# An adaptive-layernorm block of linear attention and bilinear feed-forward: reordering prepared operands, sums and loads

## The chip, the cores and the metric

The kernel runs on one core of a Trainium2 chip. The engines of a core work side by side, each through its own list of instructions in order: TensorE (PE; PEld is its weight load), VectorE (DVE), ScalarE (ACT), GpSimd (POOL) and SyncE (SP), which here only issues transfers between memory and the on-chip buffers. The metric is device microseconds (us) of one execution; the number given for a kernel is the median over its runs.

## The reference

All arrays are fp32; there are S = 2048 tokens of D = 512, 32 heads of 16, and F = 1376.

```python
mod = (_silu(c) @ w_mod).reshape(c.shape[0], 6, 1, -1)
sa, ca, ga, sb, cb, gb = (mod[:, 0], ..., mod[:, 5])
h = _layernorm(x) * (1 + ca) + sa
x = x + ga * _A_ref(h, A_wqkv, A_wo)          # linear attention
h = _layernorm(x) * (1 + cb) + sb
x = x + gb * _B_ref(h, B_w_gate, B_w_up, B_w_down)

# _A_ref: phi(t) = where(t > 0, t + 1, exp(t)) + 1e-6
kv = einsum("bhsd,bhse->bhde", phi(k), v);  z = einsum("bhsd->bhd", phi(k))
o = einsum("bhqd,bhde->bhqe", phi(q), kv) / (einsum("bhqd,bhd->bhq", phi(q), z)[..., None] + 1e-6)
# _B_ref: ((h @ w_gate) * (h @ w_up)) @ w_down
```

## The kernel before

Tokens come in four chunks (0 to 3) of four tiles of 128. To keep fp32 accuracy at the speed of the fp32r type, every operand of a matmul is split into a high part (ScalarE rounds it) and a low part (the rest, by VectorE or GpSimd: `split`, lines 195 to 197), and a product is three matmuls: high by high, high by low, low by high.

All tiles of 128 x 512 come from one pool of 94 buffers. Each tile takes a free buffer in the order in which the program is written, and the first instruction that writes it waits until the buffer's former users are through. So moving an allocation in the program changes which buffer it and later tiles get, and what they wait for. The order on each engine is the order of the program; nothing reorders it later.

*The early stage* goes over the 16 token tiles (loop from line 488): keys of the tile two ahead, the tile's part of the key sums on TensorE (L336 to L338), the sum z of all phi(k) on VectorE (L321). The table `extra` hangs further work behind some tiles: the six vectors of w_mod are loaded (`mod_load`, four tiles of 256 KB each) and summed up on VectorE one tile of weights at a time (`mod_part`, L164 and L166), and the four tiles of w_o are loaded and split. The last vector, number 5, scales the feed-forward output. At the end z is split (high on ScalarE, low on GpSimd) and summed over partitions by two matmuls (L185).

*The feed-forward* is a sequence of 19 blocks (`ffn`, `block`), 0 to 7 for chunks 0 and 1, 8 to 18 for chunks 2 and 3, one per 128 columns of F. A block multiplies the two chunks by the gate and up weights at once as a 2 x 2 matrix of halves, with seven products instead of eight. Each is six matmuls at L959. The seven are called in the order of the points at which `block` lets other work in:

```python
times(a, A["a11"], ...)                      # first product, then point "p1"
times(d, A["s1"], ...); copy(p5, d)          # second, "p5"
times(b, A["s2"], ...); copy(c, b); ...      # third, "p6"
times(a, A["a12"], ...)                      # fourth, "p2"
times(c, A["s3"], ...); p5 = c + p5          # fifth, "p7" (addition at L1018)
times(d, A["s4"], ...); u2 = d + u2          # sixth, "p3" (L1022), product with a (L987)
times(c, A["a22"], ...)                      # seventh, "p4", product with p5 (L987)
```

`copy` is ScalarE at L964, out of one accumulator bank into the next or into a tile. The fifth product adds into bank c, so it waits for the copy of the third result into c; the seventh adds into c again, so it waits until VectorE has read the fifth result at L1018. Products of a block that are still to be split into kh and kl (L196, L197) are split behind the next block's first copy. After each block come 24 matmuls of the down projection of earlier blocks (L1039 to L1041) and four additions on VectorE that take their results (evictions, L759). Weights are loaded two blocks ahead at the fifth point, and GpSimd forms their differences (L927) and low parts (L945).

The left operands for chunks 2 and 3 are prepared while blocks 1 to 8 run, by the table `plan`, keyed by block and point. The normalised tiles are written out in pieces and read back (`stow`, `unstow`); `flips` turns 32 x 32 squares on VectorE into the tile `wide` (L829); `turned(k, chunk, name)` scales and shifts one quarter of `wide` on ScalarE (L835) and so makes the *scaled block* `name` of half k: a11 and a12 come from chunk 2, a21 and a22 from chunk 3. `sums` forms on VectorE (L877) s1 = a21 + a22, s3 = a11 - a21, s2 = s1 - a11, s4 = a12 - s2, for each half k = 0, 1. `store` splits an operand and writes both parts to memory (L893); `fetch` reads them back in block 7 (L908); `split_in` splits an operand that stays on chip. The scaling of w_down's rows by the last vector is VectorE at L1104, at the third point.

Of the kernel before, what the change touches and what calls it, by code (L numbers as in the profile page):

```python
# [24 lines left out]
def tile_adaln_block(  # L25
# [12 lines left out]
    nc = tc.nc  # L38
# [3 lines left out]
    KD = D // P  # L42
# [13 lines left out]
    wo_v = wo.rearrange("(k p) n -> k p n", p=P)  # L56
# [18 lines left out]
    def T(p, tag, shape=(P, D), dt=F32, bufs=None):  # L75
        cnt[0] += 1
        return p.tile(list(shape), dt, tag="t" if p is tiles else tag, name=f"{tag}_{cnt[0]}", bufs=bufs)

    def B(tag, shape=(P, D), dt=F32):

        return T(tiles, tag, shape, dt)
# [4 lines left out]
    def bank():  # L86
        return T(ps_w, "bank")
# [25 lines left out]
    def load(src, tag):  # L113
        raw = B(tag, (P, *src.shape[1:]))[:src.shape[0]]
        nc.sync.dma_start(raw, src)
        return raw
# [4 lines left out]
    def load_mod(v):  # L121
        return [load(wm_v[:, k, v * D:(v + 1) * D], "raw") for k in range(KD)]
# [38 lines left out]
    def mod_acc(acc, raws, ks):  # L161
        for k in ks:
            if k == 0:
                nc.vector.tensor_scalar(acc, raws[k], sc[:, 0:1], None, op0=ALU.mult)  # L164
            else:
                nc.vector.scalar_tensor_tensor(acc, raws[k], sc[:, k:k + 1], acc, op0=ALU.mult, op1=ALU.add)  # L166

    def mod_col(acc, ps):

        for b in range(KD):  # L170
            nc.tensor.matmul(ps[:, b:b + 1], acc[:, b * P:(b + 1) * P], ones[:, 0:1], start=True, stop=True)
        return ps

    def col_out(v, ps, add):
        t = consts.tile([P, KD], F32, name=f"col{v}")
        nc.vector.tensor_scalar(t, ps[:, :KD], add, None, op0=ALU.add)
        return t
# [4 lines left out]
    def row_sum(pair):  # L182
        ps = bank()
        for n, x in enumerate(pair):
            nc.tensor.matmul(ps, ones_r, x, start=n == 0, stop=n == 1)  # L185
        return ps

    def mod_row(v, pair):
        ps = row_sum(pair)
        t = consts.tile([P, D], F32, name=f"row{v}")  # L190
        nc.scalar.activation(t, ps, AF.Copy)
        return t


    def split(src, h, l, low=None):
        nc.scalar.activation(h, src, AF.Copy)  # L196
        (low or nc.vector).tensor_tensor(l, src, f32(h), op=ALU.subtract)  # L197

    def split_raw(raw, shape=(P, D), low=None):
        h = B("w", shape, F32R)  # L200
        l = B("w", shape, F32R)
        split(raw, h[:raw.shape[0]], l[:raw.shape[0]], low)
        return h, l
# [255 lines left out]
    rows, cols = {}, {}  # L459
    accs = {}  # L460

    raw_m, raw_o, wo_s = {}, [], []

    def mod_load(*vs):
        raw_m.update({v: load_mod(v) for v in vs})

    def mod_part(v, *ks):
        if 0 in ks:
            accs[v] = B("f")
        mod_acc(accs[v], raw_m[v], ks)  # L470
# [4 lines left out]
             7: lambda: (wv.extend(split_raw(r) for r in raw_v[3:4]),),  # L475
             8: lambda: (mod_part(2, 0, 1), mod_load(3)),
             9: lambda: (mod_part(2, 2, 3), mod_load(4)),
             10: lambda: (pairs.update({2: split_raw(accs[2], low=nc.gpsimd)}), mod_part(3, 0, 1, 2), raw_o.extend(load(wo_v[k], "raw") for k in range(KD)), mod_load(5)),
             11: lambda: (mod_part(3, 3), mod_part(4, 0, 1), rows.update({2: mod_row(2, pairs[2])})),
             12: lambda: (mod_part(4, 2, 3), wo_s.extend(split_raw(x) for x in raw_o[:2]), cols.update({3: col_out(3, mod_col(accs[3], bank()), 0.0)})),  # L480
             13: lambda: (mod_part(5, 0, 1, 2), wo_s.extend(split_raw(x) for x in raw_o[2:]), cols.update({4: col_out(4, mod_col(accs[4], bank()), 1.0)})),
             14: lambda: (mod_part(5, 3),)}
    pairs = {}
# [343 lines left out]
    def flip(ch, *js):  # L827
        for j in js:
            nc.vector.transpose(wide[:, j].rearrange("p (m s i) -> p m s i", m=NQ, i=BL),  # L829
                                blocks.pop((ch, j)).rearrange("p (m i s) -> p m s i", m=NQ, i=BL))  # L830

    def flipped(ch, *ks):
        for k in ks:
            f = B("f")
            nc.scalar.activation(f.rearrange("p (x i) -> p x i", i=BL),  # L835
                                 wide.rearrange("p j (m s i) -> p (j m) s i", m=NQ, i=BL)[:, :, k],
                                 AF.Identity, scale=cb4[:, k:k + 1], bias=sb4[:, k:k + 1])
            blocks[ch, "f", k] = f
# [74 lines left out]
    class Right:  # L913
# [12 lines left out]
        def sums(self, on=None):  # L926
            sub = lambda out, x, y: (on or nc.gpsimd).tensor_tensor(out, x, y, op=ALU.subtract)  # L927
            b11, b12, b21, b22 = self.up[:, 0], self.up[:, 1], self.low[:, 0], self.low[:, 1]
            self.t12, self.t34 = self.tile("t"), self.tile("t")
            sub(self.t12[:, 0], b12, b11)  # L930
            sub(self.t12[:, 1], b22, self.t12[:, 0])
            sub(self.t34[:, 0], b22, b12)
            sub(self.t34[:, 1], b21, self.t12[:, 1])
# [354 lines left out]
    def turned(k, ch, n):  # L1288
        i = k + KH * (n in ("a12", "a22"))
        return lambda: (flipped(ch, i), second[k].get(n))  # L1290

    flips = lambda ch, j: lambda: flip(ch, j)
    sums = lambda k, n: lambda: second[k].sum(n)
    store = lambda k, n: lambda: second[k].aside(stash).split(n)
# [4 lines left out]
        (3, "p3"): [turned(0, 2, "a12")], (3, "p4"): [turned(1, 2, "a11"), lambda: unstow(3)],  # L1299
        (4, "p1"): [turned(1, 2, "a12")], (4, "p5"): [flips(3, 0), store(0, "a11")], (4, "p6"): [flips(3, 1)],  # L1300
        (4, "p3"): [store(0, "a12")], (4, "p4"): [flips(3, 2), store(1, "a11")],
        (5, "p1"): [flips(3, 3), store(1, "a12")], (5, "p5"): [turned(0, 3, "a21")], (5, "p6"): [turned(0, 3, "a22")],
        (5, "p3"): [sums(0, "s1")], (5, "p4"): [sums(0, "s3"), turned(1, 3, "a21")],
        (6, "p1"): [sums(0, "s2"), turned(1, 3, "a22")], (6, "p5"): [sums(0, "s4"), store(0, "s1")],
        (6, "p6"): [sums(1, "s1"), store(0, "s3")], (6, "p3"): [store(0, "s2")], (6, "p4"): [sums(1, "s3")],
        (7, "p1"): [sums(1, "s2"), split_in(1, "s1")], (7, "p5"): [sums(1, "s4"), split_in(0, "s4")],
        (7, "p6"): [split_in(1, "s2")], (7, "p3"): [split_in(1, "s3")], (7, "p4"): [split_in(0, "a22")],
        (8, "p1"): [split_in(1, "s4")], (8, "p5"): [split_in(1, "a22")]})
# [31 lines left out]
```

## Time and profile before

| | us |
|---|---|
| median of 3 runs (564.26 to 564.45) | 564.3 |
| profiled execution | 563.62 |
| its span, first to last instruction | 561.9 |
| TensorE busy | 554.7 |
| VectorE busy | 382.4 |
| ScalarE busy | 280.9 |
| GpSimd busy | 189.5 |

The granted TensorE clock of the profiled execution is 0.999 of full speed. A timeline row has the start in us from the span's start, the time that the row covers, engine, line and operation, the tile written and those read, shapes, and the number of instructions merged into the row; in brackets stands the idle time of the engine just before, and what ended it. A row of a stretch has its bounds, its length, and for each engine the busy time with the number of instructions, then the granted clock, the share of the transfer engines and GB/s. A row of transfers has the number, the size of each and the median time from issue to landing.

### The profile page before, as it was taken

How to read it: one execution, taken by the hardware profiler on the slowest of the kernel's cores; microseconds unless marked ns; L12 is line 12 of the kernel's file. 1: busy time of each engine (PE TensorE's matmuls, PEld its weight loads, DVE VectorE, ACT ScalarE, POOL GpSimd, SP SyncE). 2: the span in 40 equal slices, each digit the busy share in tenths (PEclk: the TensorE clock that was granted, in tenths of full speed). 3: DMA queues.
4: the chain of work that ended last, by engine and by line, in shares of the span. 5: the costliest groups of instructions: out<-in, count | busy, mean ns of one | idle time of the engine just before them, and what ended most of it. 6: DMA issues, size and time to landing. Idle time of an engine off the chain costs nothing. (4 is left out here: it accounts for less than half of the span.)

```text
span 561.9 us, 7305 instructions
## 1 busy us (share of the span) xinstructions
PE 554.7 (99%) x2539; PEld 454.5 (81%) x2539; DVE 382.4 (68%) x629; ACT 280.9 (50%) x503; POOL 189.5 (34%) x195
## 2 busy tenths in 40 slices
PE   8999999999999999999999999999999999999997
PEld 7788888888888778878887887787888888888886
DVE  7896968787969876769877587786444444344435
ACT  4695866456557546354783545554333333334120
POOL 2000000100011300001598665656667446446200
PEclk9999999999999999999999999999999999999999
DMA  8900212400501001814425142491335222200004
GB/s 287 384 2 2 75 52 98 152 0 2 153 3 76 0 1 40 259 37 114 132 69 155 41 168 95 154 341 35 114 112 151 56 58 56 58 19 1 1 0 150
DMA packets 51077, 52.01 MB, mean 93 GB/s; under 512 B 7712, under 2 KB 32544, under 8 KB 51040
## 3 DMA queue, kind: packets, MB, share of 16 engines
q1 hardware_dynamic: 51040, 51.54, 28.9%
q8 instruction: 20, 0.33, 0.2%
q14 instruction: 17, 0.14, 0.1%
HBM read 39.46 MB, written 12.06 MB: 92 GB/s over the span
## 5 line engine op out<-in xcount | busy, mean ns | idle before, releaser
L959 PE MATMUL bank<-h,w 128*128 128x512 f32 (+1 forms) x798 | 185.7, 390 | 1.5 <-ACT bank L964 0.9
L959 PEld LDWEIGHTS bank<-h,w 128*128 128x128 f32 (+1 forms) x798 | 148.1, 186 | 36.1 <-ACT bank L964 2.1
L964 ACT ACTIVATE bank<-bank 128x512 f32<-128x512 f32 (+1 forms) x38 | 22.1, 582 | 136.2 <-PE bank L959 136.2
L759 DVE TENSOR_TENSOR x<-acc,x 128x512 f32<-128x512 f32 (+1 forms) x73 | 48.7, 682 | 49.3 <-PE acc L1041 49.3
L945 POOL TENSOR_TENSOR w<-raw,w 128x256 fp32r<-128x256 f32 (+3 forms) x38 | 42.0, 1105 | 111.1 <-ACT w L938 111.1
L1039 PE MATMUL acc<-w,kh 128*128 128x512 f32 (+2 forms) x154 | 59.6, 387 | 0.0
L1040 PE MATMUL acc<-w,kh 128*128 128x512 f32 (+2 forms) x154 | 59.6, 387 | 0.0
L1041 PE MATMUL acc<-w,kl 128*128 128x512 f32 (+2 forms) x154 | 59.5, 386 | 0.0
L197 POOL TENSOR_TENSOR w<-raw,w 128x512 fp32r<-128x512 f32 (+1 forms) x25 | 35.4, 1418 | 54.3 <-ACT w L196 54.3
L237 POOL TENSOR_TENSOR rstd<-ve,half 128x4 f32<-128x4 f32 (+1 forms) x10 | 10.6, 1060 | 123.2 <-DVE ve L236 121.5
L945 POOL TENSOR_TENSOR w<-t,w 128x512 fp32r<-128x512 f32 (+1 forms) x38 | 48.9, 1308 | 0.0
L197 DVE TENSOR_TENSOR kl<-u,kh 128x512 fp32r<-128x512 f32 (+1 forms) x38 | 26.7, 744 | 31.4 <-ACT kh L196 31.4
L209 PE MATMUL bank<-w,h 128*128 128x512 f32 x104 | 40.8, 392 | 0.0
L211 PE MATMUL bank<-w,h 128*128 128x512 f32 x104 | 40.5, 390 | 0.0
L210 PE MATMUL bank<-w,h 128*128 128x512 f32 x104 | 40.5, 389 | 0.0
L695 PE MATMUL acc<-w,xh 128*128 128x512 f32 x120 | 38.2, 400 | 0.0
L1039 PEld LDWEIGHTS acc<-w,kh 128*128 128x128 f32 (+1 forms) x154 | 28.9, 188 | 6.0
L1040 PEld LDWEIGHTS acc<-w,kh 128*128 128x128 f32 (+1 forms) x154 | 28.9, 188 | 5.9
L1041 PEld LDWEIGHTS acc<-w,kl 128*128 128x128 f32 (+1 forms) x154 | 28.9, 188 | 5.9
L1018 DVE TENSOR_TENSOR u<-bank,u 128x512 f32<-128x512 f32 (+1 forms) x19 | 13.1, 687 | 28.1 <-PE bank L959 20.7
L246 ACT ACTIVATE n<-x,nmr,rstd 128x512 f32<-128x512 f32 x30 | 22.9, 804 | 16.3 <-DVE nmr L240 15.0
L196 ACT ACTIVATE w<-raw 128x512 fp32r<-128x512 f32 (+2 forms) x44 | 26.3, 618 | 1.6 <-DVE raw L739 1.0
(198 smaller groups left out, 1112.9 us busy)
## 6 DMA issues: line engine op xcount, KB each, us to landing
raw<-in_w_mod_dram SPq DMA_DIRECT2D x24, 256.0 KB, 4.0
raw<-in_B_w_down_dram SPq DMA_DIRECT2D x20, 256.0 KB, 2.9
raw<-in_B_w_gate_dram SPq DMA_DIRECT2D x36, 128.0 KB, 3.6
raw<-in_B_w_up_dram SPq DMA_DIRECT2D x36, 128.0 KB, 3.5
x<-in_A_x_dram SPq DMA_DIRECT2D x16, 256.0 KB, 5.2
out_dram<-x SPq DMA_DIRECT2D x15, 256.0 KB, 2.7
raw<-in_A_wqkv_dram SPq DMA_DIRECT2D x12, 256.0 KB, 5.2
kept<-f SPq DMA_DIRECT2D x8, 256.0 KB, 2.0
```

What stands on the lines that cost most here:

```text
L196: nc.scalar.activation(h, src, AF.Copy)
L197: (low or nc.vector).tensor_tensor(l, src, f32(h), op=ALU.subtract)
L209: nc.tensor.matmul(ps, ah, bh, start=i == 0, stop=False)
L210: nc.tensor.matmul(ps, ah, bl, start=False, stop=False)
L211: nc.tensor.matmul(ps, al, bh, start=False, stop=i == n - 1)
L695: nc.tensor.matmul(yps[i], x, y, start=False, stop=k == KD - 1 and x is al, skip_group_check=True)
L759: nc.vector.tensor_tensor(xt[:, a:b], dn[j][:, a:b], xt[:, a:b], op=ALU.add)
L945: sub = lambda out, x, y: (on or nc.gpsimd).tensor_tensor(out, x, f32(y), op=ALU.subtract)
L959: mm = lambda x, y, **kw: nc.tensor.matmul(ps, x[:, k], y, skip_group_check=True, **kw)
L1039: nc.tensor.matmul(ps, hh[:, a:b], dh[:n, c:d], start=i == 0, stop=False)
L1040: nc.tensor.matmul(ps, hh[:, a:b], dl[:n, c:d], start=False, stop=False)
L1041: nc.tensor.matmul(ps, hl[:, a:b], dh[:n, c:d], start=False, stop=i == len(hs) - 1)
```

## The change

Three things are moved; no instruction is added or taken away.

In the early stage the loads of w_o are divided, two tiles behind token tile 10 and two behind tile 11, and the four loads of vector 5 move from tile 10 to tile 12.

In the table `plan`, the scaled blocks a21 and a22 of half 0 are made behind the third and sixth product of block 5 instead of the second and third, and the split and store of a12 of half 1 move from the first point of block 5 to its seventh. The sums of half 0 follow one place later: s1 behind the seventh product of block 5, s3 and s2 behind the first and second of block 6, s4 behind the seventh. The sums s1 and s3 of half 1 stand behind the seventh product of block 6; before, s1 stood behind the third.

```diff
-             10: lambda: (pairs.update({2: split_raw(accs[2], low=nc.gpsimd)}), mod_part(3, 0, 1, 2), raw_o.extend(load(wo_v[k], "raw") for k in range(KD)), mod_load(5)),
-             11: lambda: (mod_part(3, 3), mod_part(4, 0, 1), rows.update({2: mod_row(2, pairs[2])})),
-             12: lambda: (mod_part(4, 2, 3), wo_s.extend(split_raw(x) for x in raw_o[:2]), cols.update({3: col_out(3, mod_col(accs[3], bank()), 0.0)})),
+             10: lambda: (pairs.update({2: split_raw(accs[2], low=nc.gpsimd)}), mod_part(3, 0, 1, 2), raw_o.extend(load(wo_v[k], "raw") for k in range(2))),
+             11: lambda: (mod_part(3, 3), mod_part(4, 0, 1), rows.update({2: mod_row(2, pairs[2])}), raw_o.extend(load(wo_v[k], "raw") for k in range(2, KD))),
+             12: lambda: (mod_part(4, 2, 3), wo_s.extend(split_raw(x) for x in raw_o[:2]), cols.update({3: col_out(3, mod_col(accs[3], bank()), 0.0)}), mod_load(5)),
...
-        (5, "p1"): [flips(3, 3), store(1, "a12")], (5, "p5"): [turned(0, 3, "a21")], (5, "p6"): [turned(0, 3, "a22")],
-        (5, "p3"): [sums(0, "s1")], (5, "p4"): [sums(0, "s3"), turned(1, 3, "a21")],
-        (6, "p1"): [sums(0, "s2"), turned(1, 3, "a22")], (6, "p5"): [sums(0, "s4"), store(0, "s1")],
-        (6, "p6"): [sums(1, "s1"), store(0, "s3")], (6, "p3"): [store(0, "s2")], (6, "p4"): [sums(1, "s3")],
+        (5, "p1"): [flips(3, 3)], (5, "p6"): [turned(0, 3, "a21")], (5, "p3"): [turned(0, 3, "a22")],
+        (5, "p4"): [store(1, "a12"), sums(0, "s1"), turned(1, 3, "a21")],
+        (6, "p1"): [sums(0, "s3"), turned(1, 3, "a22")], (6, "p5"): [sums(0, "s2"), store(0, "s1")],
+        (6, "p6"): [store(0, "s3")], (6, "p3"): [store(0, "s2")], (6, "p4"): [sums(0, "s4"), sums(1, "s1"), sums(1, "s3")],
```

## The prediction

> **What bounds the kernel now.** I read the page's busy times first, then the busy times in stretches (one stretch per feed-forward block of the first half), then the timelines of single engines where a stretch is longer than its neighbours.
>
> ```profile
> PE 554.7 (99%) x2539; PEld 454.5 (81%) x2539; DVE 382.4 (68%) x629; ACT 280.9 (50%) x503; POOL 189.5 (34%) x195
> ...
> 304.79:319.75 14.96, 14.96 (x68) 12.39 (x66) 9.24 (x14) 7.83 (x14) 9.87 (x12) 1.00 0.23 71
> 319.75:334.93 15.18, 15.18 (x68) 12.31 (x66) 12.59 (x18) 7.77 (x15) 9.75 (x11) 1.00 0.45 152
> 334.93:351.08 16.15, 15.30 (x68) 12.31 (x67) 10.90 (x16) 8.25 (x15) 8.69 (x9) 1.00 0.27 86
> 351.08:367.02 15.94, 15.45 (x68) 12.23 (x67) 12.89 (x19) 7.77 (x15) 10.41 (x12) 1.00 0.51 170
> 367.02:382.31 15.29, 15.29 (x68) 12.22 (x67) 11.90 (x19) 7.73 (x16) 9.16 (x10) 1.00 0.96 310
> ```
>
> The five stretches are blocks 3 to 7. TensorE is busy 99% of the span, so only its waits can be won. Each block is 66 matmuls (42 of the seven products, 24 of the down projection). Block 3 has no wait: 14.96/66 = 0.227 us per matmul, 1.36 us per product. Blocks 5 and 6, which the change edits, are 1.19 and 0.98 longer. The clock column is 1.00 throughout, so this is waiting and not a slower clock. Where it lies, from TensorE's timeline:
>
> ```profile
> 125.88 1.02 PE L185 MATMUL bank<-w,ones_r 128*128 128x512 f32 x2
> 126.74 0.40 PE L336 MATMUL acc<-kh,xh 128*128 128x512 f32 x1
> ...
> 339.69 0.84 PE L959 MATMUL bank<-h,w 128*128 128x512 f32 x3
> 341.38 0.50 PE L959 MATMUL bank<-h,w 128*128 128x512 f32 x1 [0.85 <-ACT bank L964]
> ...
> 358.75 0.84 PE L959 MATMUL bank<-h,w 128*128 128x512 f32 x3
> 360.08 0.50 PE L959 MATMUL bank<-h,w 128*128 128x512 f32 x1 [0.49 <-DVE u L1018]
> ```
>
> Block 5: the last three matmuls of the fourth product begin at 339.69, so the fifth product was due at 339.69 + 3 x 0.227 = 340.37. It began at 341.38, 1.01 late, on ScalarE's copy of the third result. Block 6: the seventh product was due at 358.75 + 0.68 = 359.43 and began at 360.08, 0.65 late, on VectorE's addition to the fifth result (L1018). The first matmul after each wait lasts 0.50, where three in a row last 0.84 = 2 x 0.227 + 0.39; so a wait costs a further 0.11. Earlier, the two matmuls of the sum for z (L185) take 126.74 - 125.88 = 0.86 where two are worth 0.45: 0.41 lost.
>
> **The change part by part.** No instruction is added or removed; the three parts reorder.
>
> *Block 5, ScalarE.* Its order before, and the flip it waits for:
>
> ```profile
> 336.55 0.58 ACT L964 ACTIVATE bank<-bank 128x512 f32<-128x512 f32 x1 [7.41 <-PE bank L959]
> 337.04 1.14 ACT L196 ACTIVATE kh<-u 128x512 fp32r<-128x512 f32 x2
> 338.08 0.62 ACT L196 ACTIVATE h<-f 128x512 fp32r<-128x512 f32 x1
> 338.60 0.59 ACT L964 ACTIVATE u<-bank 128x512 f32<-128x512 f32 x1
> 340.03 0.81 ACT L835 ACTIVATE f<-wide,sb,cb 128x512 f32<-128x512 f32 x1 [0.84 <-DVE wide L829]
> 340.75 0.58 ACT L964 ACTIVATE bank<-bank 128x512 f32<-128x512 f32 x1
> ...
> 338.91 1.09 DVE L829 STREAM_TRANSPOSE wide<-u 128x512 f32<-128x512 f32 x1
> ...
> 352.69 0.58 ACT L964 ACTIVATE bank<-bank 128x512 f32<-128x512 f32 x1 [7.05 <-PE bank L959]
> ```
>
> The copy at 340.75 is the late one. Ahead of it stands the scaled block a21 (L835), which waits 0.84 us for VectorE's last flip (338.91 + 1.09 = 340.00). The change puts the a21 block behind this copy and moves the split of a12 (the h at 338.08) behind the seventh product. ScalarE then has the copy of the first result, two kh, the copy of the second result from 338.08, and the copy of the third. A copy begins 0.26 after its product's last slot (the first product ends at 334.93 + 1.36 = 336.29, the copy begins at 336.55); the third product ends at 339.01, so its copy runs 339.27 to 339.85, 0.52 before TensorE wants it at 340.37. The wait goes with its restart: 1.01 + 0.11 = **-1.12**. The two scaled blocks (0.81 each) and the split (0.62) come to lie after the fifth and seventh products, before ScalarE's 7.05 us of idle time ahead of 352.69. That idle time is their cover; without it they would cost 2.2 us at the next block's first copy. On VectorE the low part of a12 and the sum s1 follow the seventh product, where s1 and s3 were: the same count. The a12 store's two transfers on SP now stand behind the five weight loads of this block instead of ahead, so the loads go out sooner; they were not late, so I count nothing. The stored tiles are read back two blocks later; if that were late, block 8 would wait.
>
> *Block 6, VectorE.* Its chain before, the ScalarE high part of s3 that it needs, and POOL beside it:
>
> ```profile
> 353.85 1.29 DVE L197 TENSOR_TENSOR kl<-u,kh 128x512 fp32r<-128x512 f32 x2 [1.88 <-ACT kh L196]
> 355.06 0.69 DVE L877 TENSOR_TENSOR s<-s,f 128x512 f32<-128x512 f32 x1
> 355.78 0.69 DVE L877 TENSOR_TENSOR s<-f,s 128x512 f32<-128x512 f32 x1
> ...
> 357.59 0.69 DVE L877 TENSOR_TENSOR s<-f,f 128x512 f32<-128x512 f32 x1
> 358.19 1.23 DVE L197 TENSOR_TENSOR h<-s,h 128x512 fp32r<-128x512 f32 x1
> 359.35 0.68 DVE L1018 TENSOR_TENSOR u<-bank,u 128x512 f32<-128x512 f32 x1
> ...
> 356.93 0.63 ACT L196 ACTIVATE h<-s 128x512 fp32r<-128x512 f32 x1
> ...
> 357.94 0.94 POOL L945 TENSOR_TENSOR w<-raw,w 128x256 fp32r<-128x256 f32 x1 [5.45 <-ACT w L938]
> ```
>
> VectorE starts something every 0.60 from 353.85 to 358.19, then meets POOL. Three sums stand ahead of L1018; after the change two do (s3 and s2). The low part of s3 then needs no turn behind the sum at 357.59; it may begin when its high part is done, 356.93 + 0.63 = 357.56, so in the sum's place, 357.59, and last 0.69 as the sum did. L1018 needs the fifth result: the sixth product starts at 359.43 - 1.36 = 358.07, plus 0.26 is 358.33; L1018 would run 358.33 to 359.01, 0.42 before it is wanted. The wait goes: 0.65 + 0.11 = **-0.76**. The remaining 0.22 of this block lies before the fifth product, behind a ScalarE order that the change leaves alone; it stays, as does the 0.33 of block 7.
>
> *Behind the seventh product of block 6* now stand three sums (s4, and s1 and s3 of the second half) where one stood:
>
> ```profile
> 361.26 1.11 DVE L197 TENSOR_TENSOR h<-s,h 128x512 fp32r<-128x512 f32 x1
> ...
> 362.89 1.18 DVE L877 TENSOR_TENSOR s<-f,f 128x512 f32<-128x512 f32 x1
> 365.18 2.73 DVE L759 TENSOR_TENSOR x<-acc,x 128x512 f32<-128x512 f32 x4 [1.10 <-PE acc L1041]
> 369.79 1.29 DVE L197 TENSOR_TENSOR kl<-u,kh 128x512 fp32r<-128x512 f32 x2 [1.88 <-ACT kh L196]
> ```
>
> Kept on the old clock, the first sum ends at 364.07 as now. Two more at 0.60 each end by 365.3; at the slowest, one per 1.70 (from the end of the operation at 361.26 to the end of the sum, 364.07 - 362.37), by 367.47. The four evictions (L759) then follow at 0.60, 2.5 us in all, and the next block's kl is due at 369.79 - 0.76 = 369.03, TensorE being earlier by 0.76. The fast end, 367.8, is early by 1.2; the slow end, 369.9, late by 0.9. From kl on VectorE has work without a gap up to the addition that block 7's seventh product waits for, so TensorE would pay for lateness. I take the measured 1.18 per sum: 366.4, evictions done by 368.9, in time by 0.1: **0**, bounds 0 and +0.9.
>
> The Trainium skill ("SBUF — State Buffer", section "Who interferes with whom") says that a VectorE instruction with two SBUF inputs and a GpSimd instruction that reads SBUF exclude each other, and that the second to issue is blocked until the first ends. The trace agrees: the operation at 358.19 met the POOL row of 357.94 and took 1.23 instead of 0.69. By that rule alone sums beside a backlogged POOL go to the slow end, and this term would be +0.9.
>
> *The loads of the early stage.* The rows around the sum for z:
>
> ```profile
> 104.42 0.63 ACT L196 ACTIVATE xh<-n 128x512 fp32r<-128x512 f32 x1 [4.81 <-PE acc L337]
> 110.35 0.72 ACT L327 ACTIVATE kh<-phi,eps_phi 128x512 fp32r<-128x512 f32 x1 [2.54 <-PE acc L337]
> 121.27 0.63 ACT L301 ACTIVATE h<-h 128x512 f32<-128x512 f32 x1
> 124.35 0.63 ACT L196 ACTIVATE w<-z 128x512 fp32r<-128x512 f32 x1 [2.44 <-DVE z L321]
> ...
> 105.08 0.69 DVE L197 TENSOR_TENSOR xl<-n,xh 128x512 fp32r<-128x512 f32 x1 [2.04 <-ACT xh L196]
> 118.58 0.48 DVE L164 TENSOR_SCALAR f<-raw,sc 128x512 f32<-128x512 f32 x1
> ...
> 101.62 3.12 SPq L115 DMA_DIRECT2D raw<-in_w_mod_dram  x4
> ...
> raw<-in_w_mod_dram SPq DMA_DIRECT2D x24, 256.0 KB, 4.0
> ```
>
> ScalarE stood 4.81 and 2.54 us at 104.42 and 110.35 for buffers that TensorE had not released; VectorE lost 2.04 behind the first. In the new program order neither instruction waits for those matmuls, since six, and then four, of the eight loads have not yet taken buffers. VectorE thus runs earlier, until ScalarE's exponential of a fresh TensorE result (121.27 + 0.63 = 121.90) holds it: two VectorE steps later, about 123.25, z is complete, against 124.3 now. TensorE wants the low part 0.30 earlier than it came (0.41 less the restart of 0.11), so a move of 1.1 removes the wait: **-0.41**, bounds 0 and -0.41. The last vector's first load now waits for the same matmul that 110.35 waited for: issue 110.35, landing 4.0 later, 114.4; the fourth at most 3.12 after. VectorE wants the first at 118.58 less the 2.04 gained, 116.5: 2.1 spare.
>
> Sum: -1.12 - 0.76 - 0.41 + 0 = -2.29 us. The profiled execution took 563.62 (span 561.9), which gives 561.33; the runs' median of 564.3 lies 0.68 above it, so 564.3 - 2.3 = **562.0**.
>
> **The rivals.** A measurement of this kernel tells about 0.2% (1.1 us) from no change.
>
> *POOL comes first in block 6.* VectorE leads POOL by only 357.94 - 357.59 = 0.35. Were it later, the low part would last 1.23 as it does now, L1018 would stay at its place, and the 0.76 would stay: 562.8. For it: the small lead. Against it: one operation less ahead, and the lead is set by ScalarE's order, which is unchanged.
>
> *The three sums alternate with POOL*, one per 1.70, and block 7 pays 0.9: 562.9. For it: POOL's rows around them are as long as that already; against it: two sums of the same kind cost 1.11 and 1.18.
>
> *The z part does nothing*, because another wait holds VectorE: 562.4. It speaks against this that only 0.30 of 2.04 us is needed.
>
> *The wait of block 5 is only handed on*, for example to the seventh product behind VectorE's flip and scaling: about 563.3. VectorE is through with the flip at 340.00 and the scaling one step later, long before the fifth result, so I give it little.
>
> *Slower: the last vector's tiles come late.* VectorE meets them ahead of z; with z about 0.8 earlier than needed, TensorE pays a wait W there less 0.8 and has its restart, so against gains of 1.88 and 0.41 the change loses from W = 3.0 on. If the buffers came free one token tile later than I read (110.35 - 104.42 = 5.93), the third tile (issued two thirds of 3.12 after the first) would land at 110.35 + 5.93 + 2.1 + 4.0 = 122.4. VectorE wants it two steps of 0.60 after 116.5, at 117.7: W = 4.7, 1.7 over, 566.0.
>
> **How the numbers follow.** The forecast, with all three waits gone: 0.58, own range 561.4 to 562.5. POOL first: 0.08 (562.8). Alternating sums: 0.10 (562.9; with POOL first as well 563.7). The z part nil: 0.12 (562.4). Handed on: 0.06 (563.3). Late tiles: 0.06 (566.0). Faster by over 0.2% (below 563.17) are the first four less 0.02 for two of them together: 0.86; same, those and the handed-on case: 0.08; slower, the late tiles: 0.06. The range 561.3 to 563.3 leaves out the late tiles and the double cases; its low end is what else could go of the 0.22 and 0.33 of blocks 6 and 7.
>
> **What would show it.** Block 5 at about 15.0 and block 6 at about 15.2 long; no idle time before the fifth product of block 5 or the seventh of block 6; the copy in block 5 ahead of L835; the low part of s3 at 0.69 and not 1.23; two L185 matmuls 0.45 long; evictions after block 6 ending before kl is ready. The prediction is wrong if block 7 grows beyond 15.8, if a TensorE wait on VectorE or a load appears between 111 and 127, or if block 6 keeps its 0.65.

## The result and the profile after

| us | before | after |
|---|---|---|
| median of the runs (lowest to highest) | 564.05 (563.18 to 564.45, 6 runs) | 561.15 (560.89 to 561.93, 6 runs) |
| profiled execution, its span | 563.62, 561.9 | 560.93, 559.2 |

The ratio is 0.9954, with a 95% interval of 0.9941 to 0.9967: the change takes off 1.9 to 3.3 us. Beside the experiments the kernel before was timed again, at 563.39 to 563.59 (medians). There its 10 executions with a granted clock of 0.996 or 0.997 took 564.00 to 564.59 and the 36 with 0.999 or 1.000 took 563.06 to 563.70 (median 563.33), while the four of the kernel after with 0.999 or 1.000 have the median 560.99, which is 2.33 less.

In the kernel after, the busy times by stretch, one per feed-forward block from 3 to 7 (bounds, length, then TensorE, its weight loads and the other engines as before, granted clock, transfers):

```profile
304.01:318.97 14.96, 14.96 (x68) 12.39 (x66) 9.24 (x14) 7.83 (x14) 9.87 (x12) 1.00 0.22 71
318.97:334.14 15.17, 15.17 (x67) 12.31 (x66) 12.60 (x18) 7.77 (x15) 9.74 (x11) 1.00 0.47 152
334.14:349.10 14.96, 14.96 (x67) 12.39 (x66) 11.07 (x15) 8.23 (x15) 9.06 (x9) 1.00 0.30 92
349.10:364.29 15.19, 15.19 (x67) 12.31 (x66) 12.39 (x17) 7.77 (x15) 9.29 (x9) 1.00 0.54 181
364.29:379.58 15.29, 15.29 (x67) 12.22 (x66) 13.73 (x22) 7.73 (x16) 9.84 (x10) 1.00 0.95 305
```

Block 5 went from 16.15 to 14.96 (-1.19), block 6 from 15.94 to 15.19 (-0.75); blocks 3, 4 and 7 stayed within 0.01, and so did block 8 (13.75 and 13.76), so the later store of a12 was not too late for its readers. TensorE's timeline of the same kernel, at the places where it had waited:

```profile
125.49 0.63 PE L185 MATMUL bank<-w,ones_r 128*128 128x512 f32 x2
125.96 0.39 PE L336 MATMUL acc<-kh,xh 128*128 128x512 f32 x1
...
338.22 2.65 PE L959 MATMUL bank<-h,w 128*128 128x512 f32 x11
...
353.63 5.38 PE L959 MATMUL bank<-h,w 128*128 128x512 f32 x22
```

The two matmuls of the sum for z take 125.96 - 125.49 = 0.47, up to the start of L336, instead of 0.86. In block 5 eleven matmuls from the start of the fourth product (338.22) run in one row, across the start of the fifth. In block 6 the seventh product begins inside the row of 22. So the span lost 0.39 + 1.19 + 0.75 = 2.33 at the three places, of 2.7 in all. The rest, 0.37, lies ahead of anything that was moved: a version that keeps the old loads, and the old wait, also began block 0 at 267.10, where the execution shown of before began it at 267.53. I count it as a difference between executions, and not as the change's.

Why block 5 is free, in ScalarE's timeline of the kernel after:

```profile
336.25 1.14 ACT L196 ACTIVATE kh<-u 128x512 fp32r<-128x512 f32 x2
337.30 0.59 ACT L964 ACTIVATE u<-bank 128x512 f32<-128x512 f32 x1
338.42 0.58 ACT L964 ACTIVATE bank<-bank 128x512 f32<-128x512 f32 x1 [0.54 <-PE bank L959]
338.91 0.59 ACT L964 ACTIVATE u<-bank 128x512 f32<-128x512 f32 x1
339.39 0.81 ACT L835 ACTIVATE f<-wide,sb,cb 128x512 f32<-128x512 f32 x1
```

The copy of the third result (338.42) no longer stands behind L835. ScalarE now waits 0.54 for TensorE there, and the copy is through at 339.00, 0.58 before the fifth product starts.

Why block 6 is free, in the timelines of VectorE and, last, GpSimd:

```profile
352.29 1.29 DVE L197 TENSOR_TENSOR kl<-u,kh 128x512 fp32r<-128x512 f32 x2 [2.30 <-ACT kh L196]
...
355.31 0.69 DVE L1104 TENSOR_TENSOR raw<-raw,row 128x512 f32<-128x512 f32 x1
355.91 0.69 DVE L197 TENSOR_TENSOR h<-s,h 128x512 fp32r<-128x512 f32 x1
356.51 0.69 DVE L1018 TENSOR_TENSOR u<-bank,u 128x512 f32<-128x512 f32 x1
...
360.78 1.18 DVE L877 TENSOR_TENSOR s<-f,s 128x512 f32<-128x512 f32 x1
361.88 2.78 DVE L877 TENSOR_TENSOR s<-f,f 128x512 f32<-128x512 f32 x2
364.58 2.47 DVE L759 TENSOR_TENSOR x<-acc,x 128x512 f32<-128x512 f32 x4
367.06 1.29 DVE L197 TENSOR_TENSOR kl<-u,kh 128x512 fp32r<-128x512 f32 x2
...
355.96 1.25 POOL L945 TENSOR_TENSOR w<-raw,w 128x256 fp32r<-128x256 f32 x1 [5.83 <-ACT w L938]
```

The low part of s3 (355.91) lasts 0.69 and L1018 ends at 357.20, 0.27 before the seventh product begins at 357.47. But the low part of s3 began only 0.05 before GpSimd's operation, because kl began 352.29 - 349.10 = 3.19 after the block's start and not 2.77 as before. Further down stand the three sums: 1.18 for the first, 2.78 for the two others. The evictions end at 367.05, and kl starts at 367.06, with no time to spare.

The early stage of the kernel after: two of ScalarE's waits, its split of z, VectorE's first use of the last vector and its last wait ahead of z, and the issue of that vector's loads.

```profile
104.72 0.60 ACT L191 ACTIVATE row<-bank 128x512 f32<-128x512 f32 x1 [1.51 <-PE bank L185]
...
110.19 0.63 ACT L196 ACTIVATE xh<-n 128x512 fp32r<-128x512 f32 x1 [0.42 <-PE acc L338]
...
122.87 0.63 ACT L196 ACTIVATE w<-z 128x512 fp32r<-128x512 f32 x1 [1.36 <-DVE z L321]
...
116.36 0.48 DVE L164 TENSOR_SCALAR f<-raw,sc 128x512 f32<-128x512 f32 x1
...
121.55 0.69 DVE L304 SCALAR_TENSOR_TENSOR h<-bank,h 128x512 f32<-128x512 f32 x1 [0.66 <-ACT h L301]
...
109.95 1.75 SPq L115 DMA_DIRECT2D raw<-in_w_mod_dram  x4
```

The waits of 4.81 and 2.54 for buffers have gone (one of 0.42 behind L338 is there instead, at 110.19), z is split at 122.87 instead of 124.35, and VectorE takes up the last vector at 116.36 without waiting for its loads. It even stands idle for 0.66 later on (121.55), for ScalarE.

### The profile page after: what moved, and what is told of

Read it like the earlier page. It is cut to its first block, busy times and chain, and to the rows that moved or that the text cites. A ratio compares the mean times of both kernels' runs of the same rounds, so it can differ in the third digit from the quotient of the medians.

```text
span 559.2 us, 7301 instructions
## 1 busy us (share of the span) xinstructions
PE 552.8 (99%) x2539; PEld 453.4 (81%) x2539; DVE 383.7 (69%) x629; ACT 281.0 (50%) x503; POOL 190.1 (34%) x195
## 4 chain that ended last, share of the span: by engine, by line
PE 88%; DVE 5%; ACT 2%; DMA 1%; issue 1%; POOL 1%; SPq 1%; POOLq 0%; ACTq 0%; DVEq 0%
PE bank L959 28%; PE acc L1039 6%; PE acc L1041 6%; PE acc L1040 6%; PE acc L695 5%; PE bank L209 5%; PE bank L211 5%; PE bank L210 5%; PE acc L338 3%; PE acc L337 3%; PE acc L336 3%; PE bank L772 2%; PE bank L774 2%; PE bank L773 2%; PE bank L259 2%
## 5 line engine op out<-in xcount | busy, mean ns | idle before, releaser
L945 POOL TENSOR_TENSOR w<-raw,w 128x256 fp32r<-128x256 f32 (+3 forms) x38 | 41.9, 1101 | 107.8 <-ACT w L938 107.8
L945 POOL TENSOR_TENSOR w<-t,w 128x512 fp32r<-128x512 f32 (+1 forms) x38 | 48.5, 1296 | 0.0
L1018 DVE TENSOR_TENSOR u<-bank,u 128x512 f32<-128x512 f32 (+1 forms) x19 | 13.1, 688 | 27.5 <-PE bank L959 20.7
```

## The experiments

**The two halves of the change.** One kernel takes from the change the moved loads alone, another the new table alone.

```diff
 # loads alone: before, with the three lines of `extra` as in the change
 # table alone: after, with the three lines of `extra` as before
```

> The kernel before with only the loads moved (two of w_o and the four of vector 5). My theory: the two buffer waits of ScalarE near 104 and 110 us go, z is complete about 1.1 us or more earlier, the two matmuls of the sum for z take 0.45 instead of 0.86, and nothing else changes: 0.41 us less, ratio 0.9993; blocks 5 and 6 keep 16.15 and 15.94. Rival (the loads do nothing by themselves): ratio 1.000 and the 0.86 stays.

> The changed kernel with the loads put back: only the plan of blocks 5 and 6 is changed. My theory: the parts add up, so 1.9 us less than before (ratio 0.9967), block 5 at 14.96, block 6 at 15.2, block 7 at 15.3, and the two matmuls of the sum for z at 0.86. Rival (the parts depend on each other through the buffers that the loads take): blocks 5 to 7 differ from the changed kernel's by more than 0.1.

Loads alone: 562.88, ratio 0.9992 (0.9983 to 1.0001). The two L185 matmuls take 0.47 up to L336, ScalarE's waits of 4.81 and 2.54 have gone, and blocks 5 and 6 keep their length (16.09 and 15.95). Table alone: 561.31, ratio 0.9963 (0.9951 to 0.9976); blocks 5 and 6 are 14.96 and 15.16, the two L185 matmuls take 0.88, and the waits of 4.81 and 2.54 are there. The product of the ratios is 0.9955, the whole change 0.9954: the parts add. The load part is too small to time (its interval reaches 1); that it is there rests on the traces.

**Which load move counts.**

```diff
-  10: ... raw_o.extend(load(wo_v[k], "raw") for k in range(2))),
-  11: ..., raw_o.extend(load(wo_v[k], "raw") for k in range(2, KD))),
+  10: ... raw_o.extend(load(wo_v[k], "raw") for k in range(KD))),
+  11: ...
```

> The changed kernel with the loads of w_o left together behind token tile 10, so that only the four loads of vector 5 are moved. If the move of the vector's loads alone frees the buffers in time: the two matmuls of the sum for z are 0.47 apart and the time is that of the change, 561.1. If the division of the w_o loads is needed too: they are 0.6 to 0.88 apart and the time is 561.3 to 561.5, which a measurement can hardly tell apart, so the trace decides.

561.07, ratio 0.9948 (0.9931 to 0.9965), and the two L185 matmuls take 0.46 (126.54 to 127.00). Moving the four loads of vector 5 is enough to take the wait away; dividing those of w_o adds nothing that these runs show.

**Block 5: the scaled block in its old place.**

```diff
-  (5, "p6"): [turned(0, 3, "a21")],
+  (5, "p5"): [turned(0, 3, "a21")],
```

> The changed kernel with the scaled block a21 alone put back behind the second product of block 5; the split of a12 stays late. My theory: a21 behind the flip is the whole wait, so ScalarE stands until the flip ends, the copy of the third result is about 1.0 late and block 5 is 16.0 to 16.1 long again (1.1 more than the changed kernel). Rival (ScalarE simply had too much work ahead of the copy, and the split of a12, 0.52, is half of it): block 5 grows by about 0.5 only.

562.41, ratio 0.9984 (0.9975 to 0.9994); block 5 is 16.16 again. ScalarE and TensorE in this kernel's timeline:

```profile
339.55 0.81 ACT L835 ACTIVATE f<-wide,sb,cb 128x512 f32<-128x512 f32 x1 [1.41 <-DVE wide L829]
340.27 0.57 ACT L964 ACTIVATE bank<-bank 128x512 f32<-128x512 f32 x1
...
340.89 2.34 PE L959 MATMUL bank<-h,w 128*128 128x512 f32 x9 [0.90 <-ACT bank L964]
```

The a12 split is out of ScalarE's way here, and it only makes L835 wait longer for the flip (1.41 where before it was 0.84). So the one scaled block behind the flip was the whole wait, and the rival is out. The other edit to this block is put back alone:

```diff
-  (5, "p1"): [flips(3, 3)], ... (5, "p4"): [store(1, "a12"), sums(0, "s1"), ...]
+  (5, "p1"): [flips(3, 3), store(1, "a12")], ... (5, "p4"): [sums(0, "s1"), ...]
```

> The changed kernel with the split and store of a12 of half 1 put back behind the first product of block 5. My theory: with a21 out of the way ScalarE reaches the copy of the third result in time even with this split (0.52) ahead of it, so block 5 stays at 14.96 and the move of a12 is worth nothing there. Rival (the split is also needed): block 5 grows by up to 0.5.

One execution, 560.82, block 5 at 14.96: moving the a12 store bought nothing in block 5. It did change something later. With a12 early (this kernel, before and the loads alone) kl in block 6 starts 2.77 after the block's start. Of the nine kernels with a12 late, seven (the kernel after among them) have 3.17 to 3.20, and two, those with late tiles and with three more moves, have 2.83. ScalarE's kh is at the same place in all twelve (2.11 to 2.12). What holds kl back was not found. The traces speak against a buffer that is still in use: none of the semaphores (the counters by which engines wait for each other) that kl waits for changes between 2.75 and 3.17. They show one other difference: an 8 KB packet on the queue that the profile calls "instruction" begins 3.85 to 4.18 after the block's start in all nine kernels with a12 late, and in the three others there is none in the block's first 9 us. Whether that has to do with the delay was not tested.

**Block 6: one sum in its old place.**

```diff
-  (6, "p6"): [store(0, "s3")], ... (6, "p4"): [sums(0, "s4"), sums(1, "s1"), sums(1, "s3")],
+  (6, "p6"): [sums(1, "s1"), store(0, "s3")], ... (6, "p4"): [sums(0, "s4"), sums(1, "s3")],
```

> The changed kernel with one sum, s1 of the second half, put back behind the third product of block 6. In the changed kernel the low part of s3 began 0.05 ahead of a POOL operation and VectorE's addition ended 0.27 ahead of need. Theory A (order alone): one more operation of 0.60 makes the addition 0.33 late; with the restart block 6 grows by 0.4 to 0.45. Theory B (POOL now starts first, the low part waits for it and lasts about 1.2 to 1.8): the addition is 0.9 or more late, block 6 grows by 0.9 to 1.5. In both the evictions after block 6 end earlier and block 7 does not grow.

561.55, ratio 0.9972 (0.9961 to 0.9983); block 6 is 15.72 (+0.53), block 7 15.31. VectorE and GpSimd in this kernel:

```profile
356.94 0.69 DVE L877 TENSOR_TENSOR s<-f,f 128x512 f32<-128x512 f32 x1
357.54 0.69 DVE L197 TENSOR_TENSOR h<-s,h 128x512 fp32r<-128x512 f32 x1
358.14 0.68 DVE L1018 TENSOR_TENSOR u<-bank,u 128x512 f32<-128x512 f32 x1
...
356.98 1.84 POOL L945 TENSOR_TENSOR w<-raw,w 128x256 fp32r<-128x256 f32 x1 [5.81 <-ACT w L938]
```

The sum costs its place, one step of 0.60, and the wait returns as 0.41 with a restart of 0.11. GpSimd did not get in: its operation lasted 1.84 until VectorE was through. Before the change it lasted 0.94 and VectorE's low part 1.23. That is Theory A, a little dearer than its 0.4 to 0.45. So of the 0.75 saved in block 6, 0.53 goes with the place of this one sum; the other 0.2 goes with where kl starts and how VectorE and GpSimd meet, which no run takes apart.

**Behind block 6: is there room?** A fourth sum, whose result nothing uses, is added to the three, whole and then half as wide.

```diff
   (6, "p4"): [sums(0, "s4"), sums(1, "s1"), sums(1, "s3"),
+      lambda: nc.vector.tensor_tensor(wide[:, 0], second[1].f["a11"], second[1].f["a21"], op=ALU.subtract)],
 # half: wide[:, 0, 0:256], ...["a11"][:, 0:256], ...["a21"][:, 0:256]
```

> The changed kernel with a fourth, useless sum behind the seventh product of block 6 (its result is not used). In the changed kernel the next block's first low part started 0.01 us after the evictions, with nothing to spare. My theory: the added operation costs its whole length, 0.6 if POOL is through and up to 1.2 beside POOL, and block 7 grows by that (15.9 to 16.5). Rival (VectorE was held by ScalarE's kh, and evictions have room): block 7 stays within 0.1 of 15.29.

> The useless fourth sum made half as wide (256 of 512 columns), so that it costs VectorE about 0.3 to 0.6 us instead of 1.09 and the next block's kl is late by about 0.3 to 0.5 instead of 0.93. One for one: block 7 grows from 15.29 to about 15.7 to 15.9 (the lateness and one restart of 0.11), no matmul slower, about 561.6. Step theory (a late chain meets GpSimd's low parts of weights, each VectorE operation behind them then takes 1.48 instead of 0.69): at least one operation at 1.4 or more, block 7 at 16.6 to 17.6, TensorE's wait 1.3 to 2.3. Then the clock: if a wait of 2.92 us is what brought the slow matmuls, they are absent here; if they come with any wait at this place, eight matmuls stand 0.43 us apart again. Between 562 and 563.5 by the step theory.

Half: 561.72, ratio 0.9967 (0.9954 to 0.9981). It takes 0.74 (365.82 to 366.56), more than expected, kl starts 0.70 later in its block (3.47 against 2.77), and block 7 grows from 15.29 to 15.98, by 0.69. That is one for one, without a step: there is no room behind the three sums. The stretch of block 7 in this kernel:

```profile
365.48:381.46 15.98, 15.30 (x68) 12.22 (x66) 14.56 (x23) 7.84 (x16) 11.45 (x11) 1.00 0.91 301
```

TensorE is busy for 15.30 of it, so the rest, 0.68, is waiting, at the full clock.

Whole: 565.73, ratio 1.0038 (1.0024 to 1.0052), and block 7 is 19.83, 4.54 longer for one operation of 1.09. The rival is out, and the theory, with 16.5 at most, is far off too. VectorE, GpSimd and TensorE of this kernel:

```profile
368.30 1.28 DVE L197 TENSOR_TENSOR kl<-u,kh 128x512 fp32r<-128x512 f32 x2
...
371.31 1.08 DVE L197 TENSOR_TENSOR h<-s,h 128x512 fp32r<-128x512 f32 x1
372.32 1.49 DVE L1104 TENSOR_TENSOR raw<-raw,row 128x512 f32<-128x512 f32 x1
373.73 1.48 DVE L197 TENSOR_TENSOR h<-s,h 128x512 fp32r<-128x512 f32 x1
375.13 0.68 DVE L1018 TENSOR_TENSOR u<-bank,u 128x512 f32<-128x512 f32 x1
...
371.23 0.62 POOL L945 TENSOR_TENSOR w<-raw,w 128x192 fp32r<-128x192 f32 x1 [4.22 <-ACT w L938]
...
375.87 2.47 PE L959 MATMUL bank<-h,w 128*128 128x512 f32 x6 [2.92 <-DVE u L1018]
378.13 0.63 PE L1039 MATMUL acc<-w,kh 128*128 128x512 f32 x1
378.55 0.63 PE L1040 MATMUL acc<-w,kh 128*128 128x512 f32 x1
```

kl is 0.93 later in its block. Then GpSimd gets in, and three operations that last 0.69 elsewhere take 1.08, 1.49 and 1.48, together 2.0 more. TensorE waits 2.9 longer than in the kernel after, and afterwards eight matmuls stand about 0.42 apart instead of 0.227: 1.6. That makes the 4.5. In the stretch from 376 to 380 the clock column has 0.57:

```profile
376.00:380.00 4.00, 4.00 (x11) 3.17 (x12) 3.27 (x5) 0.00 (x0) 3.61 (x5) 0.57 0.62 174
```

**Late tiles, the rival on the slower side.** The loads of vector 5 are put behind an added store of a 256 KB tile one token tile later, so that they really are late.

```diff
-  12: ... , mod_load(5)),
-  13: lambda: (mod_part(5, 0, 1, 2), ...
+  12: ... ),
+  13: lambda: (nc.sync.dma_start(tc.dram_tile([P, D], F32, name="held"), phk[15]), mod_load(5), mod_part(5, 0, 1, 2), ...
```

> The changed kernel with the four tiles of vector 5 loaded behind a store that needs VectorE's result of about 115.8, so about 6 us later than in the changed kernel (one added store of 256 KB). It measures the price of the slower case. My theory: the loads go out from about 116.3, the third tile lands near 121.3, VectorE stands about 3.9 us (W), and TensorE waits W - 0.85 at the second matmul of the sum for z: 3.0, with the restart 3.1 more than the changed kernel, ratio to the kernel before about 1.001. Rival (VectorE's 3.49 us of idle time at 127 takes it up): TensorE waits less than 1.

563.83, ratio 1.0007 (0.9998 to 1.0017): the whole gain is gone. The issue of the loads, VectorE's waits, and TensorE in this kernel:

```profile
116.44 2.17 SPq L115 DMA_DIRECT2D raw<-in_w_mod_dram  x4
...
119.69 0.49 DVE L164 TENSOR_SCALAR f<-raw,sc 128x512 f32<-128x512 f32 x1 [3.10 <-DMA raw<-in_w_mod_dram]
120.35 0.75 DVE L166 SCALAR_TENSOR_TENSOR f<-raw,sc,f 128x512 f32<-128x512 f32 x1 [0.17 <-DMA raw<-in_w_mod_dram]
121.87 0.75 DVE L166 SCALAR_TENSOR_TENSOR f<-raw,sc,f 128x512 f32<-128x512 f32 x1 [0.77 <-DMA raw<-in_w_mod_dram]
...
127.01 0.50 PE L185 MATMUL bank<-w,ones_r 128*128 128x512 f32 x1 [1.21 <-ACT w L196]
128.36 0.50 PE L185 MATMUL bank<-w,ones_r 128*128 128x512 f32 x1 [0.85 <-POOL w L197]
128.70 0.39 PE L336 MATMUL acc<-kh,xh 128*128 128x512 f32 x1
```

VectorE waits 3.10 + 0.17 + 0.77 = 4.04. TensorE reaches L336 at 128.70 instead of 125.64 + 0.45 = 126.09, so it loses 2.6, where 3.1 was expected, and 1.4 less than VectorE. So the slower side was real in kind: about two thirds of such a wait is paid. It did not happen because the loads were issued at 109.95, 6.4 before VectorE needed the first.

**The waits that the change leaves.** The same kind of edit is made at three further places.

```diff
-  (2, "p5"): [flips(2, 0)],
+  (2, "p3"): [flips(2, 0)],
-  (6, "p5"): [sums(0, "s2"), store(0, "s1")], (6, "p6"): [store(0, "s3")],
+  (6, "p5"): [sums(0, "s2")], (6, "p6"): [store(0, "s1"), store(0, "s3")],
-  (7, "p6"): [split_in(1, "s2")], (7, "p3"): [split_in(1, "s3")], (7, "p4"): [split_in(0, "a22")],
+  (7, "p3"): [split_in(1, "s2")], (7, "p4"): [split_in(1, "s3"), split_in(0, "a22")],
```

> The changed kernel with three more moves of the same kind: the split of s1 in block 6 behind the third result's copies (was ahead of them), the split of s2 of half 1 in block 7 behind the sixth product (was third) with that of s3 behind the seventh, and the first flip of block 2 behind the sixth product (was second). My theory: each takes one operation from ahead of a wait of TensorE: block 6 shorter by 0.17 (15.02), block 7 by 0.24 (15.05), block 2 by 0.43 (15.04); 0.84 less than the changed kernel, ratio to the kernel before about 0.9945. Rival (the moved work is handed on to the evictions or to the next block): one of the blocks 3, 7 or 8 grows by what is gained.

560.12 (559.82 to 560.26), ratio 0.9938 (0.9926 to 0.9951), span 558.4. Blocks 2, 6 and 7 of this kernel by stretch:

```profile
288.73:303.69 14.96, 14.96 (x67) 12.39 (x66) 12.39 (x14) 7.74 (x15) 14.88 (x14) 1.00 0.58 158
348.78:363.76 14.98, 14.98 (x67) 12.39 (x66) 12.42 (x17) 7.77 (x15) 9.09 (x9) 1.00 0.53 173
363.76:378.85 15.09, 15.09 (x67) 12.22 (x66) 14.54 (x22) 7.84 (x16) 10.17 (x11) 1.00 0.97 322
```

Block 2 lost 0.51, block 6 0.21 and block 7 0.20, against the kernel after, where 0.43, 0.17 and 0.24 were expected. Blocks 3 and 8 keep 14.96 and 13.75, so nothing was handed on. This version is faster than both kernels: its slowest execution (560.26) lies below the fastest of the kernel after (560.89), which was timed earlier, and the three blocks are worth 0.92.

## Why the prediction was right

- *Block 5, -1.12*: measured -1.19, and shown to be the place of a21 by putting it back (+1.20). The prediction named the move of the a12 split beside it; putting that back alone cost nothing. The copy was through 0.58 before it was wanted, forecast 0.52. The prediction has the two scaled blocks between the fifth and the seventh product; they came to lie behind the third and the sixth, at 339.39 and 342.49, which changed nothing.
- *Block 6, -0.76*: measured -0.75. One step on the way failed, "the lead is set by ScalarE's order, which is unchanged": ScalarE's kh did keep its place, but kl started 0.42 later, and the lead on GpSimd was 0.05 and not 0.35. It cost nothing: with a12 early the lead is 0.35, as forecast, and block 6 is 15.18 against 15.19. The delay of 0.4 appears only in kernels with the a12 store behind the seventh product, which the prediction counted at nothing, but not in all of them.
- *Three sums, 0*: the forecast was "in time by 0.1" and it was 0.01. The size of a sum was off: the two in one row take 2.78, 1.78 and 1.08 each, where 2 x 1.18 was taken. That the end came out all the same is luck. The half sum shows that this zero was an edge: 0.70 of lateness cost 0.69. The upper bound of +0.9 was no bound either, since it counted lateness one for one: a lateness of 0.93 cost 4.5.
- *The sum for z, -0.41*: measured -0.39. z came 1.1 us sooner against TensorE, 0.8 more than the 0.3 that was needed. The loads alone show it, and the table alone keeps the wait.
- *Late tiles*: the loads were issued at 109.95, forecast 110.35, and VectorE's first use was at 116.36, forecast 116.5. The rival's price was put at the wait less 0.8, and a restart; it was the wait less 1.5 and a restart of 0.1, which fits the 0.66 us that VectorE stands idle at 121.55 in the kernel after and that absorbs a part as well. The wait from which the change would lose moves from 3.0 to about 3.7.
- *The total*: -2.29 was forecast. The three places measure -2.33, as do the executions at the same granted clock, and the medians of the table differ by 2.9. The median forecast, 562.0, and the low end of its range, 561.3, started from 564.3; that is the long side of the kernel before (its later medians are 563.39 to 564.05), and so the median of 561.15 lies 0.15 below the range. Against the profiled execution the sum gave 561.33 and 560.93 was measured; the 0.40 between them is mostly the 0.37 ahead of anything that was moved.
- *The other rivals*: nothing was handed on from block 5, since blocks 7 and 8 kept their lengths. By the prediction's own terms that case would be 562.0 + 1.12 = 563.1, not the 563.3 that it gives.
- *Left in place*: 0.22 in block 6 and 0.33 in block 7 stayed, as forecast. The last kernel shows that most of them could go too.

## What to carry to other kernels

When the busiest engine waits behind an in-order engine, find the instruction ahead of the late one that has itself a late input, and move that one behind; here 0.81 us of scaling cost TensorE 1.1 us only because it waited for a flip. Count the room at the place where the work goes, not only at the place that it leaves: three sums fitted behind block 6 with 0.01 us to spare, and a fourth lost more than the whole change gained (4.6 against 2.9). A load that takes a pooled buffer early can hold up work that has nothing to do with it, so look at which waits end on an old user of a buffer.

## What the runs showed of the hardware

**Who gets in, VectorE or GpSimd.** In the twelve traces there are 15 meetings in blocks 6 and 7 in which a GpSimd low part (L945) becomes ready while VectorE runs operations of 0.69 with two SBUF inputs back to back, one every 0.60. In 11 of them GpSimd's start is recorded 0.04 to 0.25 after the start of the VectorE operation under way: it then waits through all that follow (the 1.84 above; 2.19 in the kernel with the half sum). In the other four it is 0.32 to 0.52 after: GpSimd gets in, and VectorE's next operation lasts 1.08 to 1.23. No case lies between. So a shift of a tenth of a microsecond decides. In block 6 of the kernel after GpSimd came 0.65 after the start of L1104 and 0.05 after that of s3's low part; 0.13 to 0.33 earlier it would have been as late behind L1104 as those four. The Trainium skill ("SBUF — State Buffer", section "Who interferes with whom") says that the one that issues first holds the shared ports and the other is blocked. The exclusion agrees; that the earlier GpSimd operation is the one that waits through several later VectorE operations is more than the section says, if the recorded starts are taken for the issue.

**The clock after a wait.** The wait of 2.92 us in the kernel with the whole sum was followed by eight matmuls about 0.42 us apart, 3.4 us at little over half the rate, with the granted clock at 0.57 in the stretch. After the waits of 1.21 and 0.85 us in the kernel with late tiles only the first matmul was longer, 0.50 for 0.39, and block 7 of the kernel with the half sum, where TensorE waited 0.68, has 1.00 throughout. The Trainium skill ("TensorE: Matmul & The Clock Gate", section "What's actually happening") gives an idle window of about 3.4 us after which the clock is halved; here the clock fell behind a wait shorter than that, in one place of one kernel, and how long an idle time it takes was not measured. Nor is a wait the only thing that goes with it. In the profiled executions with one sum early, with the half sum and with the loads of vector 5 alone, the granted clock is 0.50 to 0.53 from 16 to 18 us of the span, where TensorE had waited 0.18 to 0.32 us at about 10 us; in the kernel after it is 1.00 there, behind a wait of 0.60 at the same place.
